# Soft-MoE over a windowed average: first output batch in half sets, later row softmaxes one batch later

## The chip, the cores and the metric

The kernel runs on one core of a Trainium2 chip. The metric is the device time of one execution in microseconds (us), lower is better. The core's engines work side by side and wait for each other through semaphores: TensorE (PE, its weight loads PEld), VectorE (DVE), ScalarE (ACT), GpSimd (POOL) and SyncE (SP), which here issues all loads of the inputs x, w1, w2 and all stores of the output. Sixteen DMA engines move the data. DVE and ACT copy results out of PSUM, the memory that TensorE writes.

## The reference

```
# x: 8 x 3584 x 192, weight: 8 x 7, phi: 192 x 32, w1: 8 x 192 x 1024, w2: 8 x 1024 x 192
w = softmax(weight, axis=-1)                        # one 7-tap filter for each of 8 heads of 24 channels
x = causal_window_sum(w, x).reshape(28672, 192)     # 28672 tokens
logits = x @ phi                                    # 28672 x 32
d = softmax(logits, axis=0)                         # over all tokens
slot_input = (d.T @ x).reshape(8, 4, 192)           # 8 experts, 4 slots each
for e in range(8):
    slot_out[e] = relu(slot_input[e] @ w1[e]) @ w2[e]
c = softmax(logits, axis=1)                         # over the 32 slots of a token
out = c @ slot_out                                  # 28672 x 192, float32
```

## The kernel before

The eight batches of 3584 tokens go through three stages. **Stage 1** (to some 126 us) loads x, filters it on TensorE, forms the logits of all batches (tiles `eb[b]`, 128 partitions by 896) and gathers the slot inputs. **Stage 2** (126 to 143 us) runs the experts: two layers on TensorE, whose result lies in PSUM (`op`, 128 by 2 by 192). It is copied to SBUF in two halves `oc[0]` (DVE) and `oc[1]` (ACT), multiplied with a selector (`gather`) and copied by DVE to `so`, the slot outputs. **Stage 3** (from 143 us) is the output. For a batch b, `c @ slot_out` needs `so` and the row softmax of `eb[b]`, which the key `ct{b}` stands for.

`rows(b)` makes that softmax in eight steps in a row: DVE transpose (L615), DVE minimum (L612), POOL subtraction (L605), ACT exponential (L618), DVE sum (L612), two short DVE steps (L608, L609), POOL multiplication (L605), DVE transpose (L622).

The output of a batch is 4 groups c of 128 rows by 7 tokens q by 192 values. A **set** of the loop at the end of the kernel takes two tokens k, k+1 of all four groups (the fourth set one token): 8 products (16 PE instructions in the profile; 56 for a batch) into two PSUM tiles, c = 0, 1 in the first and c = 2, 3 in the second. Two pairs of PSUM tiles take turns. Each PSUM tile is copied to the output buffer `ob` by ACT or DVE, 768 values wide (L197 for ACT, L201 for DVE). The buffers `ob` of batches 0 to 3 are the former x tiles `rb[1]` to `rb[4]`, used again by batches 4 to 7. After the last set of a batch, SP issues four stores, one for each c, of 7 tokens (672 KB). Batch 0 is cut finer: its first set is copied in four pieces 384 wide and stored at once (four stores of 2 tokens, 192 KB), and the other five tokens follow after the last set (four stores of 480 KB).

The order of the work on each engine is fixed before the run. Every step is given to `Plan.add` with a modelled cost for each engine that could do it, what it reads and writes, and a priority. Steps below priority 1000 are placed first; the rest (the row softmaxes and the output) fill the gaps in the order of their priority, the smaller first. The row softmaxes of batches 0 to 2 have priorities 1100 to 1120, and those of later batches

```python
pr = 1100 + 10 * b if b < 3 else 2000 + 20 * (b - 2) - 1
```

where the output of batch b has 2000 + 20 b + k. So the softmax of batch 3 stands just ahead of the output of batch 1. Waits are put in by the framework, which keeps two engines from working on the same PSUM tile at once.

Of the kernel before, what the change touches and what calls it, by code (L numbers as in the profile page):

```python
# [15 lines left out]
class Plan:  # L16
# [15 lines left out]
    def add(self, fn, cost, reads=(), writes=(), prio=0.0, after=(), chain=False):  # L32

        i = len(self.steps)
        deps = {self.writer[r] for r in reads if r in self.writer}
        if chain:
            if self.last is not None:
                deps.add(self.last)
            self.last = i
        for w in tuple(writes) + tuple(after):  # L40
            if w in self.writer:
                deps.add(self.writer[w])
            deps.update(self.readers.get(w, ()))
        for r in reads:
            self.readers.setdefault(r, []).append(i)
        for w in writes:
            self.writer[w] = i
            self.readers[w] = []
        deps.discard(i)
        self.steps.append((fn, cost, deps, prio))  # L50
# [101 lines left out]
def tile_conv_softmoe(ctx: ExitStack, tc: tile.TileContext, x, weight, phi, w1, w2, out):  # L152
    nc = tc.nc
    P = 128
    B, S, D = x.shape
# [8 lines left out]
    NU = S // T // 2  # L164
# [5 lines left out]
    TQ = NC // P  # L170
# [10 lines left out]
    add = plan.add  # L181

    def act(n):
        return 0.2 + n / 1250

    def dve(n):
        return 0.13 + n / 960

    def pool(n):
        return 0.12 + n * 0.00217  # L190

    def dma(nbytes):
        return {"DMA": nbytes / 320e3}

    def copy(e, dst, src):
        if e == "ACT":
            nc.scalar.copy(dst, src)  # L197
        elif e == "POOL":
            nc.gpsimd.tensor_copy(dst, src)  # L199
        else:  # L200
            nc.vector.tensor_copy(dst, src)  # L201

    def veng(e):
        return nc.gpsimd if e == "POOL" else nc.vector
# [4 lines left out]
    def sb(name, *shape):  # L209
        return cp.tile(list(shape), F32, tag=name, name=name)  # L210

    prs = [pp.tile([P, 2, 512], F32, tag=f"ps{i}", name=f"ps{i}") for i in range(4)]
# [25 lines left out]
    so = sb("so", P, D)  # L238
# [64 lines left out]
    for i in range(5):  # L303
        if i == 1:
# [7 lines left out]
                start=True, stop=True,  # L312
# [32 lines left out]
    for h in range(H):  # L345
# [7 lines left out]
        def bsum(e, prod=prod, h=h):  # L353
# [7 lines left out]
            writes=[f"prod{h}"], prio=-40 + h,  # L361
# [19 lines left out]
    def take():  # L381
        p = state["pair"]
        while p in state["held"]:
            p = (p + 1) % 4
        state["pair"] = (p + 1) % 4
        return p
# [207 lines left out]
            load_x(b + NR)  # L594

    def rows(b):
        pr = 1100 + 10 * b if b < 3 else 2000 + 20 * (b - 2) - 1
        fl = eb[b]
        ev = fl.rearrange("p (q n) -> p q n", n=NS)
        rm = rms[:, b % 2]  # L600
        rb_ = rm.unsqueeze(2).broadcast_to((P, 28, NS))
        ks = [f"e{b}.0", f"e{b}.1"]

        def apply_rows(op):
            return lambda e: veng(e).tensor_tensor(out=ev, in0=ev, in1=rb_, op=op)  # L605

        def recip(e):
            nc.vector.tensor_scalar(out=rm, in0=rm, scalar1=1e-9, scalar2=None, op0=ALU.add)  # L608
            nc.vector.reciprocal(rm, rm)  # L609

        def red(op):
            return lambda e: nc.vector.tensor_reduce(out=rm, in_=ev, axis=AX.X, op=op)  # L612

        rk = f"rm{b % 2}"
        add(lambda e: nc.vector.transpose(fl, fl), {"DVE": dve(NC)}, writes=ks, prio=pr)  # L615
        add(red(ALU.min), {"DVE": dve(NC)}, reads=ks, writes=[rk], prio=pr)
        add(apply_rows(ALU.subtract), {"POOL": pool(NC)}, reads=[rk], writes=ks, prio=pr)
        add(lambda e: nc.scalar.activation(fl, fl, AF.Exp, scale=-1.0), {"ACT": act(NC)}, writes=ks, prio=pr)  # L618
        add(red(ALU.add), {"DVE": dve(NC)}, reads=ks, writes=[rk], prio=pr)
        add(recip, {"DVE": 0.25}, writes=[rk], prio=pr)  # L620
        add(apply_rows(ALU.mult), {"POOL": pool(NC)}, reads=[rk], writes=ks, prio=pr)
        add(lambda e: nc.vector.transpose(fl, fl), {"DVE": dve(NC)}, reads=ks, writes=[f"ct{b}"], prio=pr)  # L622
# [4 lines left out]
    for j, unit in enumerate(units):  # L627
        prev = units[j - 1] if j else []
        for s, b in enumerate(unit):
            between = {}  # L630
            if s == 0 and prev:
                step, done = logits(prev)
                if True:
                    k = 0
# [84 lines left out]
    xh = [xt[:, z].rearrange("p a b c -> p (a b c)") for z in range(2)]  # L719
# [15 lines left out]
    for q in range(4):  # L735
        for z in range(2):
            home, kk = (xh[0], xk0) if z == 0 else (flat(rb[0]), allk(0))
# [6 lines left out]
    for b in range(B):  # L744
        rows(b)

    pr = 300
    pa, pb, pc, pd = (take() for _ in range(4))
    hT = xh[1][:, 2 * NU * 32 : 3 * NU * 32].rearrange("p (q j n) -> p q j n", q=4, n=P)
    hs = xh[1][:, 3 * NU * 32 : 4 * NU * 32].rearrange("p (q f) -> p q f", f=FQ)  # L750
    oc = [xh[1][:, 4 * NU * 32 + a * D : 4 * NU * 32 + (a + 1) * D] for a in range(2)]
# [37 lines left out]
    op = prs[pc][:, 1, 0 : 2 * D].rearrange("p (a d) -> p a d", d=D)  # L789
# [47 lines left out]
    def l2(q):  # L837
        def fn(e):
            for j in range(2):
                for g in range(G):  # L840
                    nc.tensor.matmul(
                        op[g * NS : (g + 1) * NS], hT[:, q, j, g * NS : (g + 1) * NS],
                        w2v[g // 2][:, 2 * (g % 2) : 2 * (g % 2) + 2, q, j, :],
                        start=(q == 0 and j == 0), stop=(q == 3 and j == 1),
                    )

        add(
            fn, {"PE": 1.33}, reads=[f"hT{q}"] + [f"w2.{q}.{z}" for z in range(2)],
            writes=["op"], after=[f"p{pc}"] if q == 0 else [], prio=pr + 1, chain=True,
        )  # L850
# [11 lines left out]
    turn_h(3)  # L862
    for q in range(1, 4):
        l2(q)
    for a in range(2):
        add(
            lambda e, a=a: copy(e, oc[a], op[:, a]), {"ACT": 0.36} if a else {"DVE": 0.33},
            reads=["op"], writes=[f"oc{a}"], after=["dn0.0", "dn0.1"], prio=pr + 4,
        )

    def gather(e):
        for a in range(2):
# [6 lines left out]
    obk = {0: allk(1), 1: allk(2), 2: allk(3) + w1k[0], 3: allk(4) + w1k[1]}  # L879
    obv = [t[:, 0 : 4 * TQ * D].rearrange("p (c q d) -> p c q d", c=4, d=D) for t in sv]  # L880
    nset = 0
    for b in range(B):
        pr = 2000 + 20 * b
        ob = obv[b % 4]
        for k in range(0, TQ, 2):
            qs = range(k, min(k + 2, TQ))
            nq = len(qs)
            v = nset % 2
            q4 = prs[2 * v : 2 * v + 2]
            pk = [f"p{2 * v}", f"p{2 * v + 1}"]  # L890
            nset += 1

            def mm(e, qs=qs, q4=q4, b=b, k=k):
                for q in qs:
                    for c in range(4):
                        sl = slice(32 * c, 32 * c + 32)
                        cb = eb[b][sl].rearrange("p (m q) -> p m q", q=TQ)
                        nc.tensor.matmul(  # L898
                            q4[c // 2][:, c % 2, (q - k) * D : (q - k + 1) * D], cb[:, :, q], so[sl, :],
                            start=True, stop=True, tile_position=(32 * c, 0),  # L900
                        )

            add(
                mm, {"PE": 0.4 * nq}, reads=["so", f"ct{b}"],
                writes=pk + (["op", "ht0", "ht1", "mtb"] if b == 0 else []), prio=pr + k,
            )
            w = 1 if b == k == 0 else 2
            for j in range(4 // w):

                def oev(e, j=j, q4=q4, nq=nq, k=k, ob=ob, w=w):  # L910
                    c0 = j * w
                    copy(
                        e, ob[:, c0 : c0 + w, k : k + nq, :].rearrange("p c q d -> p c (q d)"),
                        q4[c0 // 2][:, c0 % 2 : c0 % 2 + w, 0 : nq * D],
                    )

                add(
                    oev, {"ACT": act(w * nq * D), "DVE": dve(w * nq * D)}, reads=[pk[j * w // 2]],
                    writes=[f"ob{b % 4}.{c}.{k}" for c in range(j * w, j * w + w)],
                    after=obk[b] if b < 4 else [], prio=pr + k,  # L920
                )
            if (b == 0 and k == 0) or k == 6:
                k0 = 2 if b == 0 and k == 6 else 0
                for c in range(4):

                    def st(e, c=c, b=b, ob=ob, k0=k0, k1=k + nq):
                        ih, f = (c // 2, c % 2) if b < NHB else (c % 2, c // 2)
                        base = (b * S + (S // 2) * ih + T * f + k0) * D
                        dst = bass.AP(out.tensor, base, ap=[[2 * T * D, 16], [TQ * D, T // TQ], [1, (k1 - k0) * D]])
                        nc.sync.dma_start(dst, ob[:, c, k0:k1].rearrange("p q d -> p (q d)"))  # L930

                    add(
                        st, dma(P * (k + nq - k0) * D * 4),
                        reads=[f"ob{b % 4}.{c}.{z}" for z in range(k0, k + nq, 2)], prio=pr + k + 4,
                    )

    plan.emit()
# [28 lines left out]
```

## Time and profile before

| what | us |
|---|---|
| median of 3 runs (204.8, 206.45, 208.21) | 206.45 |
| the profiled execution | 207.46 |
| its span from the first to the last instruction | 205.7 |
| TensorE busy in the span | 172.8 |
| VectorE busy | 151.9 |
| ScalarE busy | 100.4 |
| GpSimd busy | 78.2 |

The profiled execution took 1.76 us more than its span. Its PE row counts pipelined matmuls, so a busy PE isn't a PE at its peak. Of 60.08 MB moved, 22.02 MB are the output.

### The profile page before, as it was taken

The numbers are of one execution on the slowest core, as the hardware profiler recorded it, in microseconds if no ns is written. First come the engines' busy times: TensorE is split into PE (matmuls) and PEld (weight loads), VectorE is DVE, ScalarE is ACT, GpSimd is POOL, SyncE is SP. The second block draws the span as 40 slices with busy tenths as digits, with TensorE's granted clock in tenths as the row PEclk, the third lists the DMA queues.
The fourth block names the chain that finished last, engine by engine and source line by source line (L and its number), as shares of the span: only waits on it lengthen the run. The fifth ranks groups of instructions, "written<-read, shape, count | busy, mean of one in ns | idle before, by whom it ended". The sixth has DMA issues, their size and how long they took to land.

```text
span 205.7 us, 6098 instructions
## 1 busy us (share of the span) xinstructions
PE 172.8 (84%) x2610; PEld 104.0 (51%) x2610; DVE 151.9 (74%) x232; ACT 100.4 (49%) x156; POOL 78.2 (38%) x69
## 2 busy tenths in 40 slices
PE   7899899799999899989999999998999989970000
PEld 3367564147433385323632577344889968870000
DVE  5999971399997799959889567869799999760000
ACT  3547750391653845637873080132598878650000
POOL 7555555566665532383000303306336345300000
PEclk9999999999999999999999999999999985695555
DMA  5999999999999819998069799900599999999995
GB/s 163 323 322 330 320 330 321 330 319 316 327 323 323 252 25 291 335 379 185 20 219 317 180 384 376 358 21 0 153 304 331 407 413 412 401 413 417 414 417 211
DMA packets 46124, 60.08 MB, mean 292 GB/s; under 512 B 1682, under 2 KB 38930, under 8 KB 46098
## 3 DMA queue, kind: packets, MB, share of 16 engines
q1 hardware_dynamic: 45888, 59.68, 87.8%
q8 instruction: 20, 0.33, 0.7%
q10 hardware_dynamic: 210, 0.02, 0.1%
q14 instruction: 6, 0.05, 0.1%
HBM read 37.68 MB, written 22.02 MB: 290 GB/s over the span
## 4 chain that ended last, share of the span: by engine, by line
PE 58%; SPq 11%; DMA 8%; DVE 6%; ACT 3%; issue 2%; POOL 1%; DVEq 0%; ACTq 0%
PE ps L403 14%; PE ps L898 14%; PE ps L487 11%; PE ps L578 10%; SPq L271 9%; DMA rb<-in_x_dram 5%; PE ps L553 4%; DMA out_dram<-rb 3%; SPq L267 2%; DVE eb L511 2%; PE ps L795 2%; ACT rb L197 2%; ACT xt L526 2%; DVE rb L201 1%; DVE eb L615 1%
## 5 line engine op out<-in xcount | busy, mean ns | idle before, releaser
L197 ACT COPY rb<-ps 128x768 f32<-128x768 f32 (+1 forms) x98 | 70.1, 778 | 52.5 <-PE ps L403 27.1
L447 DVE STREAM_TRANSPOSE xt<-rb 128x1024 f32<-128x1024 f32 (+1 forms) x60 | 56.9, 1002 | 6.1 <-ACT rb L197 3.9
L199 POOL COPY rb<-rb 8x1536 f32<-8x1536 f32 x30 | 43.7, 1458 | 37.6 <-DMA rb<-in_x_dram 35.1
L403 PE MATMUL ps<-rb,toep 64*64 64x384 f32 (+1 forms) x640 | 48.4, 428 | 2.8 <-issue 1.1
L605 POOL TENSOR_TENSOR eb<-eb,rms 128x896 f32<-128x896 f32 x16 | 27.0, 1696 | 41.5 <-DVE rms L609 37.1
L898 PE MATMUL ps<-so,eb 32*128 32x192 f32 x448 | 39.2, 450 | 2.3 <-ACT rb L197 0.8
L898 PEld LDWEIGHTS ps<-so,eb 32*128 32x128 f32 x448 | 35.6, 317 | 5.9 <-issue 2.2
L403 PEld LDWEIGHTS ps<-rb,toep 64*64 64x64 f32 x640 | 21.9, 132 | 27.4 <-issue 14.8
L487 PE MATMUL ps<-xt,phi 32*32 32x448 f32 x768 | 28.7, 545 | 2.6 <-issue 2.5
L201 DVE COPY rb<-ps 128x768 f32<-128x768 f32 (+1 forms) x32 | 25.1, 816 | 4.2 <-PE ps L898 2.2
L487 PEld LDWEIGHTS ps<-xt,phi 32*32 32x32 f32 x768 | 10.1, 103 | 18.2 <-issue 12.5
L578 PE MATMUL ps<-rb,xt 128*32 128x192 f32 x448 | 19.0, 327 | 0.0
L612 DVE TENSOR_REDUCE rms<-eb 128x28 f32<-128x896 f32 x16 | 17.0, 1065 | 0.0
L578 PEld LDWEIGHTS ps<-rb,xt 128*32 128x32 f32 x448 | 14.1, 110 | 4.0 <-ACT rb L197 0.3
L526 ACT ACTIVATE xt<-eb,nmr 128x896 f32<-128x896 f32 x8 | 8.3, 1044 | 6.5 <-DVE eb L511 6.3
L197 ACT COPY xt<-ps 128x512 f32<-128x512 f32 (+2 forms) x12 | 6.1, 528 | 8.2 <-DVE xt L201 6.8
L553 PE MATMUL ps<-ident,xt 128*128 128x128 f32 x64 | 8.7, 280 | 1.3 <-ACT xt L526 1.2
L553 PEld LDWEIGHTS ps<-ident,xt 128*128 128x128 f32 x64 | 6.9, 141 | 5.6 <-ACT xt L526 3.8
L622 DVE STREAM_TRANSPOSE eb<-eb 128x896 f32<-128x896 f32 x8 | 8.9, 1107 | 0.5 <-POOL eb L605 0.5
L618 ACT ACTIVATE eb<-eb 128x896 f32<-128x896 f32 x8 | 7.6, 955 | 1.9 <-POOL eb L605 1.9
L310 PE MATMUL ps<-ident 128*128 128x512 f32 x10 | 7.4, 888 | 1.4 <-POOL ident masks.py:199 1.4
L615 DVE STREAM_TRANSPOSE eb<-eb 128x896 f32<-128x896 f32 x8 | 8.5, 1081 | 0.0
(90 smaller groups left out, 111.7 us busy)
## 6 DMA issues: line engine op xcount, KB each, us to landing
out_dram<-rb SPq DMA_DIRECT2D x28, 672.0 KB, 9.0
rb<-in_x_dram SPq DMA_DIRECT2D x24, 768.0 KB, 9.5
rb<-in_x_dram SPq DMA_DIRECT2D x8, 672.0 KB, 7.3
rb<-in_moe_w_dram SPq DMA_DIRECT2D x4, 1024.0 KB, 9.2
xt<-in_moe_w_dram SPq DMA_DIRECT2D x4, 768.0 KB, 6.0
rb<-in_moe_w_dram SPq DMA_DIRECT2D x4, 768.0 KB, 10.7
rb<-in_moe_w_dram SPq DMA_DIRECT2D x4, 512.0 KB, 13.2
out_dram<-rb SPq DMA_DIRECT2D x4, 480.0 KB, 6.2
```

The costliest lines, as they stand in the source:

```text
L197: nc.scalar.copy(dst, src)
L199: nc.gpsimd.tensor_copy(dst, src)
L201: nc.vector.tensor_copy(dst, src)
L271: nc.sync.dma_start(rb[i][:, u0 : u0 + k, :], src)
L403: nc.tensor.matmul(dst[:, :, h * CG : (h + 1) * CG], toep[r, h0 + h, :], rb[i][r, lo + g : lo + n : 2, ch], start=True, stop=True,)
L447: nc.vector.transpose(xt[:, s, k, lo : lo + n], rb[i][:, lo : lo + n, 32 * k : 32 * k + 32])
L487: nc.tensor.matmul(q[a % 2][32 * c : 32 * c + 32, a // 2, 0 : m * U * TH].rearrange("p (s u j) -> p s u j", s=m, j=TH), phi4[sl, k, :], xt ...
L553: nc.tensor.transpose(q[:, u // 4, (u % 4) * P : (u % 4 + 1) * P], t[:, u].rearrange("p g t -> p (g t)"), ident)
L578: nc.tensor.matmul(q[32 * c : 32 * c + 32, 0, 0:D], d[:, u, 32 * c : 32 * c + 32], rb[i][:, U * c + u, :], start=(u == 0), stop=(u == U - 1),)
L605: return lambda e: veng(e).tensor_tensor(out=ev, in0=ev, in1=rb_, op=op)
L612: return lambda e: nc.vector.tensor_reduce(out=rm, in_=ev, axis=AX.X, op=op)
L898: nc.tensor.matmul(q4[c // 2][:, c % 2, (q - k) * D : (q - k + 1) * D], cb[:, :, q], so[sl, :], start=True, stop=True, tile_position=(32 * ...
```

## The change

There are three edits. The output of batch 0 is made in four half sets: c = 0, 1 with tokens 0 to 3, c = 2, 3 with tokens 0 to 3, then the same with tokens 4 to 6. In a half set the first PSUM tile holds the first two tokens and is copied by ACT, the second holds the rest and is copied by DVE, one copy for each c. Each c is stored as soon as its tokens of the half set are copied: four stores of 4 tokens (384 KB) and four of 3 tokens (288 KB), in place of four of 2 and four of 5. Secondly, the row softmax of a batch b from 3 on gets the priority just ahead of batch b-1 instead of b-2. Thirdly, the expert result is copied out of PSUM by one DVE copy of 384 values in place of a DVE and an ACT copy of 192.

```diff
     def rows(b):
-        pr = 1100 + 10 * b if b < 3 else 2000 + 20 * (b - 2) - 1
+        pr = 1100 + 10 * b if b < 3 else 2000 + 20 * (b - 1) - 1
...
-    for a in range(2):
-        add(
-            lambda e, a=a: copy(e, oc[a], op[:, a]), {"ACT": 0.36} if a else {"DVE": 0.33},
-            reads=["op"], writes=[f"oc{a}"], after=["dn0.0", "dn0.1"], prio=pr + 4,
-        )
+    add(
+        lambda e: nc.vector.tensor_copy(xh[1][:, 4 * NU * 32 : 4 * NU * 32 + 2 * D], prs[pc][:, 1, 0 : 2 * D]),
+        {"DVE": 0.53}, reads=["op"], writes=["oc0", "oc1"], after=["dn0.0", "dn0.1"], prio=pr + 4,
+    )
...
-        for k in range(0, TQ, 2):
-            qs = range(k, min(k + 2, TQ))
-            nq = len(qs)
+        if b:
+            sets = [(range(4), k, min(k + 2, TQ)) for k in range(0, TQ, 2)]
+        else:
+            sets = [((c, c + 1), k, min(k + 4, TQ)) for k in (0, 4) for c in (0, 2)]
+        for cs, k, k1 in sets:
...
+            def home(c, q, q4=q4, b=b, k=k):
+                t, j = (c // 2, c % 2) if b else ((q - k) // 2, c % 2)
+                return q4[t][:, j, (q - k) % 2 * D : ((q - k) % 2 + 1) * D]
...
+                parts = [
+                    (ob[:, c, z : min(z + 2, k1), :].rearrange("p q d -> p (q d)"), q4[(z - k) // 2][:, c % 2, 0 : (min(z + 2, k1) - z) * D],
+                     (min(z + 2, k1) - z) * D, (z - k) // 2, (c,), z, ("ACT", "DVE")[(z - k) // 2])
+                    for c in cs for z in range(k, k1, 2)
+                ]
...
-            if (b == 0 and k == 0) or k == 6:
-                k0 = 2 if b == 0 and k == 6 else 0
-                for c in range(4):
+            if b == 0 or k1 == TQ:
+                for c in cs:
```

How this moves instructions is shown at three places. In the rows below, eb_73 to eb_80 are the logits of batches 0 to 7, rb_68 to rb_71 the four output buffers, ps_63 to ps_66 the four PSUM tiles. The first place is VectorE at the end of stage 2, the difference of the two orders.

```order
 L615 STREAM_TRANSPOSE eb_78<-eb_78 128x896
-L201 COPY xt<-ps_66 128x192
+L866 COPY xt<-ps_66 128x384
 L622 STREAM_TRANSPOSE eb_75<-eb_75 128x896
-L876 COPY so<-ps_65 128x192
+L875 COPY so<-ps_65 128x192
 L612 TENSOR_REDUCE rms<-eb_77 128x28
```

The copy of the expert result is twice as wide there; between it and the copy to `so` stands, as before, the last softmax step of batch 2. The second place is VectorE in the output of batches 0 and 1, before:

```order
L201 COPY rb_68<-ps_63 128x384
L201 COPY rb_68<-ps_64 128x384
L201 COPY rb_68<-ps_66 128x2x384
L201 COPY rb_68<-ps_64 128x2x384
L201 COPY rb_68<-ps_66 128x2x192
L612 TENSOR_REDUCE rms<-eb_76 128x28
L608 TENSOR_SCALAR rms<-rms 128x28
L609 RECIPROCAL rms<-rms 128x28
L201 COPY rb_69<-ps_65 128x2x384
L615 STREAM_TRANSPOSE eb_79<-eb_79 128x896
L622 STREAM_TRANSPOSE eb_76<-eb_76 128x896
L201 COPY rb_69<-ps_65 128x2x192
```

and with the change:

```order
L201 COPY rb_68<-ps_64 128x384 x2
L201 COPY rb_68<-ps_66 128x384 x2
L201 COPY rb_68<-ps_64 128x192 x2
L201 COPY rb_68<-ps_66 128x192 x2
L201 COPY rb_69<-ps_64 128x2x384
L201 COPY rb_69<-ps_66 128x2x384
L201 COPY rb_69<-ps_64 128x2x384
L201 COPY rb_69<-ps_66 128x2x192
L612 TENSOR_REDUCE rms<-eb_76 128x28
L608 TENSOR_SCALAR rms<-rms 128x28
L609 RECIPROCAL rms<-rms 128x28
L201 COPY rb_70<-ps_65 128x2x384
```

The sum of batch 3 (eb_76) and what follows it now stand behind the copies of batch 1 (rb_69) and among those of batch 2 (rb_70). The third place is SP's stores of the first batches, before:

```order
L280 DMA rb_67<-in_moe_w_dram 128x4x384
L930 DMA out_dram<-rb_68 16x8x384 x4
L930 DMA out_dram<-rb_68 16x8x960 x4
L930 DMA out_dram<-rb_69 16x8x1344 x4
L930 DMA out_dram<-rb_70 16x8x1344 x4
```

and with the change:

```order
L280 DMA rb_67<-in_moe_w_dram 128x4x384
L936 DMA out_dram<-rb_68 16x8x768 x4
L936 DMA out_dram<-rb_68 16x8x576 x4
L936 DMA out_dram<-rb_69 16x8x1344 x4
L936 DMA out_dram<-rb_70 16x8x1344 x4
```

Batch 0 has eight stores in both; the last number is the values of one row, 768 for 4 tokens and 576 for 3.

## Rows read from the trace of the kernel before

**Rows 1.** Page, part 2: GB/s moved in 40 slices of 5.14 us.

```profile
GB/s 163 323 322 330 320 330 321 330 319 316 327 323 323 252 25 291 335 379 185 20 219 317 180 384 376 358 21 0 153 304 331 407 413 412 401 413 417 414 417 211
```

**Rows 2.** Windows of stage 3: busy us of each engine, clock, DMA share, GB/s.

```profile
144.80:149.10 4.30, 3.92 (x52) 3.46 (x50) 3.81 (x6) 2.33 (x4) 0.78 (x1) 1.00 0.61 183
149.10:153.70 4.60, 4.51 (x59) 4.06 (x56) 4.50 (x8) 4.39 (x7) 1.70 (x1) 1.00 0.98 317
153.70:157.50 3.80, 3.80 (x50) 3.55 (x46) 3.65 (x6) 3.59 (x6) 1.20 (x1) 1.00 0.91 278
157.50:202.00 44.50, 25.11 (x284) 22.68 (x282) 24.05 (x33) 19.90 (x29) 10.58 (x7) 0.69 1.02 411
```

**Rows 3.** Windows of one microsecond each, with the same columns.

```profile
145.00:146.00 1.00, 0.71 (x10) 0.58 (x8) 1.00 (x3) 0.95 (x2) 0.58 (x1) 1.00 0.00 0
146.00:147.00 1.00, 1.00 (x20) 1.00 (x18) 0.69 (x1) 0.26 (x1) 0.00 (x0) 1.00 0.81 218
148.00:149.00 1.00, 1.00 (x16) 1.00 (x18) 1.00 (x3) 0.00 (x0) 0.00 (x0) 1.00 0.91 300
152.00:153.00 1.00, 0.91 (x8) 0.69 (x6) 0.97 (x2) 1.00 (x3) 0.01 (x1) 1.00 0.98 376
```

**Rows 4.** Timeline, SP's stores: start, us, and at the end how many remain.

```profile
144.83 50.51 SPq L930 DMA_DIRECT2D out_dram<-rb  x36
...
146.87 48.47 SPq L930 DMA_DIRECT2D out_dram<-rb  x33
...
147.95 47.40 SPq L930 DMA_DIRECT2D out_dram<-rb  x32
...
153.74 41.60 SPq L930 DMA_DIRECT2D out_dram<-rb  x28
...
159.00 36.34 SPq L930 DMA_DIRECT2D out_dram<-rb  x24
```

**Rows 5.** Chain that ended last, 141 to 152 us: start, us, what.

```profile
141.06 0.36 DVE xt L201
141.42 1.02 DVE eb L622
...
142.46 0.37 DVE so L876
...
142.96 1.32 PE ps L898 x16
...
144.29 0.49 ACT rb L197
...
144.80 0.57 DVE rb L201
...
147.68 4.68 PE ps L898 x55
```

**Rows 6.** Timeline, DVE in the output of batch 1.

```profile
148.51 1.08 DVE L612 TENSOR_REDUCE rms<-eb 128x28 f32<-128x896 f32 x1
149.62 0.18 DVE L608 TENSOR_SCALAR rms<-rms 128x28 f32<-128x28 f32 x1
149.84 0.33 DVE L609 RECIPROCAL rms<-rms 128x28 f32<-128x28 f32 x1
...
150.91 1.10 DVE L615 STREAM_TRANSPOSE eb<-eb 128x896 f32<-128x896 f32 x1
152.04 1.11 DVE L622 STREAM_TRANSPOSE eb<-eb 128x896 f32<-128x896 f32 x1
153.07 0.52 DVE L201 COPY rb<-ps 128x384 f32<-128x384 f32 x1
```

**Rows 7.** Groups by form from 142.9 us: count, busy us, mean ns, idle before.

```profile
L605 POOL TENSOR_TENSOR eb<-eb,rms 128x896 f32<-128x896 f32 x9 | 15.2, 1695 | 19.5 <-DVE rms L609 18.1 <-DVE rms L612 1.3
L201 DVE COPY rb<-ps 128x768 f32<-128x768 f32 x15 | 13.9, 942 | 3.2 <-PE ps L898 2.2 <-issue 0.8
...
L201 DVE COPY rb<-ps 128x384 f32<-128x384 f32 x10 | 5.1, 532 | 1.0 <-ACT rb L197 1.0
```

More of the change, by code (lines that the diff above doesn't have):

```diff
@@ L891, in tile_conv_softmoe, with mm @@
             nset += 1
-            def mm(e, qs=qs, q4=q4, b=b, k=k):
-                for q in qs:
-                    for c in range(4):
+            def home(c, q, q4=q4, b=b, k=k):
+                t, j = (c // 2, c % 2) if b else ((q - k) // 2, c % 2)
+                return q4[t][:, j, (q - k) % 2 * D : ((q - k) % 2 + 1) * D]
+            def mm(e, cs=cs, b=b, k=k, k1=k1, home=home):
+                for q in range(k, k1):
+                    for c in cs:
                         sl = slice(32 * c, 32 * c + 32)
@@ L898, in mm @@
                         nc.tensor.matmul(
-                            q4[c // 2][:, c % 2, (q - k) * D : (q - k + 1) * D], cb[:, :, q], so[sl, :],
-                            start=True, stop=True, tile_position=(32 * c, 0),
+                            home(c, q), cb[:, :, q], so[sl, :], start=True, stop=True, tile_position=(32 * c, 0),
                         )
             add(
-                mm, {"PE": 0.4 * nq}, reads=["so", f"ct{b}"],
+                mm, {"PE": 0.8}, reads=["so", f"ct{b}"],
@@ L905, in tile_conv_softmoe @@
                 writes=pk + (["op", "ht0", "ht1", "mtb"] if b == 0 else []), prio=pr + k,
             )
[L907 to L915, printed above, removed]
-                add(
-                    oev, {"ACT": act(w * nq * D), "DVE": dve(w * nq * D)}, reads=[pk[j * w // 2]],
-                    writes=[f"ob{b % 4}.{c}.{k}" for c in range(j * w, j * w + w)],
-                    after=obk[b] if b < 4 else [], prio=pr + k,
-                )
@@ L922, in tile_conv_softmoe @@
-            if (b == 0 and k == 0) or k == 6:
-                k0 = 2 if b == 0 and k == 6 else 0
-                for c in range(4):
-                    def st(e, c=c, b=b, ob=ob, k0=k0, k1=k + nq):
+            if b:
+                n = (k1 - k) * D
+                parts = [
+                    (ob[:, 2 * j : 2 * j + 2, k:k1, :].rearrange("p c q d -> p c (q d)"), q4[j][:, :, 0:n], 2 * n, j, (2 * j, 2 * j + 1), k, None)
+                    for j in range(2)
+                ]
+            else:
+                parts = [
+                    (ob[:, c, z : min(z + 2, k1), :].rearrange("p q d -> p (q d)"), q4[(z - k) // 2][:, c % 2, 0 : (min(z + 2, k1) - z) * D],
+                     (min(z + 2, k1) - z) * D, (z - k) // 2, (c,), z, ("ACT", "DVE")[(z - k) // 2])
+                    for c in cs for z in range(k, k1, 2)
+                ]
@@ new lines, in tile_conv_softmoe, with st @@
+            for dst, src, m, t, pcs, z, eng in parts:
+                cost = {"ACT": act(m), "DVE": dve(m)}
+                add(
+                    lambda e, dst=dst, src=src: copy(e, dst, src), {eng: cost[eng]} if eng else cost, reads=[pk[t]],
+                    writes=[f"ob{b % 4}.{c}.{z}" for c in pcs], after=obk[b] if b < 4 else [], prio=pr + k,
+                )
+            if b == 0 or k1 == TQ:
+                for c in cs:
+                    def st(e, c=c, b=b, ob=ob, k0=0 if b else k, k1=k1):
@@ L930, in st @@
                         nc.sync.dma_start(dst, ob[:, c, k0:k1].rearrange("p q d -> p (q d)"))
+                    k0 = 0 if b else k
                     add(
-                        st, dma(P * (k + nq - k0) * D * 4),
-                        reads=[f"ob{b % 4}.{c}.{z}" for z in range(k0, k + nq, 2)], prio=pr + k + 4,
+                        st, dma(P * (k1 - k0) * D * 4),
+                        reads=[f"ob{b % 4}.{c}.{z}" for z in range(k0, k1, 2)], prio=pr + k + 4,
                     )
```

## The prediction, made before the change was run

> **What bounds the kernel now.** I read the page by slices first. From 160 us to the end the core moves 401 to 417 GB/s slice after slice, and nothing else is left but the output; in the four slices from 144 us it is 153, 304, 331 and 407 [rows 1]. So stage 3 is bound by the stores once they run full, and its loss lies at its head. The windows give the size of it: 183, 317 and 278 GB/s in three stretches from 144.8 to 157.5 us, then 411 for 44.5 us, while the DMA engines are at 1.02 of their time [rows 2]. Computation isn't the bound later: from 157.5 on PE, DVE and ACT are busy 25.1, 24.1 and 19.9 of 44.5 us [rows 2].
>
> Next I read the issues of the stores. The first leaves at 144.83 us, the fifth (5 tokens) at 147.95, the ninth (batch 1) at 153.74, the thirteenth (batch 2) at 159.00 [rows 4]. Nothing moves before 146 us [rows 3], so some 1.3 us lie between an issue and its data. Batch 0 is 22.02/8 = 2.752 MB, and at 411 GB/s that is 6.70 us; from 146.1 it could be gone by 152.8, but its bytes come late (0.79 MB in the first four stores) and batch 1's data start only at 153.74 + 1.3 = 155.0. Up to 157.5 us the kernel has moved 4.3 x 183 + 4.6 x 317 + 3.8 x 278 = 3301 KB [rows 2].
>
> The chain before it shows what sets the first store: DVE's copy of the expert result (0.36), the last softmax step of batch 2 (1.02), `so` (0.37), 16 PE instructions (1.32), one ACT copy (0.49) [rows 5]. DVE's own first copy starts only when ACT's has ended, 144.80 against 144.29 + 0.49 [rows 5].
>
> **The change, part by part.** *One copy of the expert result.* The DVE copy is 384 wide, 0.53 us by the group of that width [rows 7] in place of 0.36. The ACT copy goes, but `gather` doesn't set the time: behind the DVE copy stands the transpose of batch 2 and behind that `so`, all on DVE without a gap [rows 5]. So `so` comes 0.17 us later, not sooner, and PE's first output product starts at 142.96 + 0.2 = 143.15. Bounds: 0 if the transpose had been waiting for something else, 0.21 with the 0.57 of the chain's DVE copy [rows 5]. I take 0.2.
>
> *Half sets.* Batch 0 keeps its 56 PE instructions, 1.32/16 = 82 ns each [rows 5]: half sets of 16, 16, 12 and 12 end at 144.5, 145.8, 146.8 and 147.8. A store needs an ACT and a DVE copy, now out of different PSUM tiles, so neither waits for the other. The DVE copy is the later one, for its tile is filled last: 144.5 + 0.55 gives the first store at 145.1, 0.25 later than before but with 384 KB in place of 192. The copies rise from 10 to 16 in batch 0, which costs 2 x 532 - 942 = 122 ns for a pair on DVE [rows 7]; they lie beside PE, which needs 1.0 to 1.3 us for a half set against two copies of 0.53 us on DVE and two of like length on ACT (0.49 for one [rows 5]). SP sends the first four in (146.87 - 144.83)/3 = 0.68 us each [rows 4], so the eight leave between 145.1 and 149.9; before, the four heavier ones left only from 147.95 on [rows 4].
>
> How fast do they move? Rows of 2 tokens move 300 GB/s at a share of 0.91, rows of 5 tokens 376 at 0.98 [rows 3], which is 330 and 384 GB/s at full share. Rows of 4 and 3 tokens lie between: 2.752 MB take 7.2 to 8.3 us from 145.1 + 1.3 = 146.4, and batch 0 is gone between 153.6 and 154.7.
>
> Here a rule speaks against any gain. The Trainium skill, "DMA: Bandwidth & Descriptors", section "Anatomy of one DMA", fits a DMA as a fixed 2.0 us plus its bytes at 436 GB/s (there for GpSimd's path), and "Rules for kernel authors" asks for 1 MiB or more in each. By that fit batch 0's eight stores cost an estimated 22.3 us before and after alike, since count and bytes stay, and nothing would be won. The trace speaks against a serial fixed cost: 218 to 300 GB/s went by while four stores of 192 KB followed each other 0.68 us apart [rows 3, 4].
>
> *Row softmaxes one batch later.* Before, DVE does steps of batches 3 and 4 around its first copy of batch 1, from the sum at 148.51 to the transpose that starts at 152.04 and takes 1.11 us, and batch 1's last copy starts only then, at 153.07 [rows 6]; its store leaves at 153.74. Now batch 1's copies are alone. But PE sets them nearly as late: 56 instructions at 4.68/55 = 85 ns [rows 5] are 4.8 us, from 147.8 to 152.5. The last copy (0.53) follows, and the ninth store leaves at 153.1, 0.65 us sooner; its data start at 154.4. So most of the DVE time that is freed is not on the path: PE is next, at 0.65 us. The steps aren't saved, only moved behind it: sum, two short steps, transpose (1.11) [rows 6] and POOL's product (1.70) [rows 7] are now due before batch 3, and the last copy of batch 2 stands behind that transpose.
>
> **The sum.** By 157.5 us the changed kernel has moved batch 0's 2752 KB, and from 154.4 on 3.1 us of batch 1. If that runs as slowly as the restart did before, at 278 GB/s, it is 862 KB; if at 411, 1274 KB [rows 2]. That makes 3614 to 4026 KB against 3301, so 313 to 725 KB less are left, and at 411 GB/s that is 0.76 to 1.76 us. I take the middle, 1.26 us, as batch 0's data end within 0.8 us of batch 1's start on either side. After that both kernels run full. The profiled execution took 207.46 us, 1.76 more than its span of 205.7, and nothing of the change touches that: 206.2. It lies 1.0 above the median of 206.45, so against the median I forecast 206.45 - 1.26 = 205.2 us.
>
> **The rivals.** *No gain (206.1).* Batch 1's stores are due where they were, because PE or the last copies hold them: then its data start at 155.0, and by 157.5 there are 2752 + 2.5 x 278 = 3447 KB, 146 more, or 0.36 us. For it: PE ends batch 1 at 152.4 before (147.68 + 4.68) and 152.5 after, and the first copy is later. Against: the row of the last copy, which stood idle for DVE's transpose [rows 6]. The page's fit above would land here too.
>
> *Full from the start (203.4).* Batch 0 runs at 411 GB/s from 146.4 and batch 1 joins without a seam: 11.1 x 411 = 4562 KB by 157.5, 1261 more, 3.07 us. For it: the issue pace of 384 KB in 0.68 us is 578 GB/s, more than the engines take. Against: rows 3, where shorter rows move less at the same share, and the first stretch, which never ran full.
>
> *Slower (207.7).* The softmax of batch 3 arrives late and starves the queue. The last DVE copy of batch 2, which two of its stores wait for, comes behind a sum (1.08), two short steps (0.51), a transpose of batch 4 (1.10) and batch 3's own (1.11), which waits for POOL's 1.70 [rows 6, 7], and a copy (0.94). From 153.05 that is 157.8 and the copy ends at 158.3. The queue has batch 1 until 154.4 + 6.7 = 161.1, so these stores must leave by 159.8: a margin of 1.5 us. A slip of 1.5 + 1.26 = 2.8 us eats the gain; with 4 us it is 206.45 + 1.2. For it: GpSimd's and ACT's steps in that chain wait for DVE, and DVE is at 0.98 of its time in the second stretch [rows 2]. Against: before, the same chain stood in front of batch 1 and the queue was empty then; now it has a full batch more. Later there is room: after 157.5 us DVE and ACT are busy for little more than half of the time [rows 2], so a chain that begins one batch's 4.8 us of PE later need not bind.
>
> **How the numbers follow.** The forecast has a chance of 0.58, no gain 0.22, full 0.12, slower 0.08. The likeliest is 205.2. The three runs of before lie 1.7 us to either side of their median, more than the bounds of the sum; with the rivals' ends the range is 203.1 to 207.0, which leaves out the slower case and the far ends of noise. A measurement of this kernel tells about 2% (4.1 us) from no change. The whole loss at the head is 12.7 x 411 - 3301 = 1919 KB, 4.7 us, and 1.3 us of it pass before the first data, so faster by over 2% needs more than there is to win: 0.03. Slower by 2% needs the starving of the third rival three times over: 0.03. Within 2%: 0.94.
>
> **What would show it.** Right: the first store at 145.1, the ninth near 153.1, the thirteenth before 159.8; above 1.2 MB by 149.1 and some 3.8 MB by 157.5 us; 411 GB/s from there on; PE's first output product 0.2 us later. DVE's copies of batch 0 no longer wait for ACT's. Wrong in the first step: the ninth store at 153.7 or later, with PE waiting for PSUM. Wrong in the second: the four-token stores move under 300 GB/s, or the rate falls again at batch 1 as it did at 153.7. Wrong in the last: a dip of GB/s after 161 us with SP waiting for a DVE copy behind L622.

## The result, and the profile after

The changed kernel takes 207.99 us against 206.79 for the kernel before, medians of 20 runs each: a ratio of 1.006 (95% interval 1.0035 to 1.0084). It is slower by 0.6%, where 0.6% faster was forecast, and 207.99 lies outside the range of 203.1 to 207.0. The profiled execution took 208.68 us, its span is 206.9. The ratios compare runs within 1.5% of each kernel's fastest one; since single runs scatter by as much, the table of the experiments has the medians of all runs beside them, and a difference that only one of the two says is called open.

The page of the changed kernel, part 2, the rows of the clock and of GB/s:

```profile
PEclk9999999999999999999999999999799975587555
...
GB/s 162 324 320 329 321 329 321 329 320 321 324 321 328 226 35 316 341 352 166 19 276 288 207 378 373 313 9 0 124 333 304 417 408 415 413 402 415 414 414 211
```

From the slice at 160 us on the rate is what it was [rows 1]: the tail still runs full. The loss lies in the slices from 144 us (124, 333, 304 against 153, 304, 331), and PEclk, the granted clock of TensorE in tenths, has a 7 there. The windows of stage 3, with the bounds of [rows 2]:

```profile
144.80:149.10 4.30, 4.22 (x54) 3.98 (x52) 2.57 (x6) 3.10 (x8) 0.95 (x1) 0.67 0.31 76
149.10:153.70 4.60, 4.55 (x62) 4.34 (x64) 3.83 (x6) 2.81 (x5) 0.00 (x0) 1.00 1.01 343
153.70:157.50 3.80, 3.80 (x53) 3.44 (x52) 3.68 (x7) 3.00 (x5) 1.70 (x1) 1.00 0.96 293
157.50:202.00 44.50, 25.46 (x282) 22.36 (x280) 25.61 (x34) 22.87 (x35) 11.84 (x7) 0.70 1.01 406
```

By 157.5 us it has moved 4.3 x 76 + 4.6 x 343 + 3.8 x 293 = 3018 KB, against 3301 before and 3614 to 4026 forecast. The start of the last window is slow as well. The changed kernel, and below it the kernel before:

```profile
157.50:160.50 3.00, 2.01 (x34) 1.96 (x32) 3.00 (x4) 2.62 (x5) 0.00 (x0) 1.00 0.98 330
160.50:202.00 41.50, 23.45 (x252) 20.41 (x248) 22.61 (x31) 20.25 (x31) 11.84 (x7) 0.67 1.02 412
```

```profile
157.50:160.50 3.00, 3.00 (x44) 2.92 (x42) 2.77 (x4) 2.28 (x4) 2.15 (x2) 1.00 1.01 403
160.50:202.00 41.50, 22.11 (x246) 19.75 (x244) 21.28 (x30) 17.62 (x26) 8.43 (x5) 0.67 1.02 412
```

That is (403 - 330) x 3.0 = 219 KB behind 157.5 us, on top of the 3301 - 3018 = 283 KB before it. Together 502 KB are 1.22 us at 411 GB/s, as much as lies between the two profiled executions (208.68 - 207.46), and about the 1.20 between the medians. Single microseconds of the changed kernel:

```profile
147.00:148.00 1.00, 1.00 (x18) 0.97 (x12) 0.79 (x2) 0.60 (x2) 0.00 (x0) 0.68 0.34 80
148.00:149.00 1.00, 0.92 (x13) 0.71 (x12) 0.76 (x3) 0.99 (x3) 0.00 (x0) 1.00 0.87 203
...
157.00:158.00 1.00, 0.55 (x8) 0.31 (x4) 0.95 (x2) 1.00 (x2) 0.25 (x1) 1.00 1.03 221
160.00:161.00 1.00, 1.00 (x17) 0.80 (x13) 0.96 (x2) 1.00 (x2) 0.00 (x0) 1.00 1.01 414
```

A share of 0.34 in the first of these says that data starts at about 147.66 us. The microsecond at 157 stands where batch 1's 7-token rows, whose first store left at 154.96 us (below), take over from batch 0's 3-token rows: the DMA engines are busy throughout (1.03), and move 221 GB/s. At 160 us the rate is full.

SP's stores, in the columns of [rows 4], are the first, fourth, fifth, eighth, ninth and thirteenth:

```profile
146.46 49.01 SPq L936 DMA_DIRECT2D out_dram<-rb  x36
...
148.76 46.71 SPq L936 DMA_DIRECT2D out_dram<-rb  x33
...
149.88 45.59 SPq L936 DMA_DIRECT2D out_dram<-rb  x32
...
153.20 42.27 SPq L936 DMA_DIRECT2D out_dram<-rb  x29
...
154.96 40.51 SPq L936 DMA_DIRECT2D out_dram<-rb  x28
...
159.78 35.69 SPq L936 DMA_DIRECT2D out_dram<-rb  x24
```

The first leaves 1.4 us later than forecast (145.1) and 1.6 later than before. The chain that ended last (start, us, what) says why:

```profile
140.99 0.56 DVE xt L866
141.54 1.02 DVE eb L622
...
142.62 0.37 DVE so L875
...
143.13 4.06 PE ps L903 x38
...
147.21 1.03 DVE rb L201 x2
...
148.29 4.10 PE ps L903 x54
...
152.41 1.42 DVE rb L201 x2
```

Between `so` and the next copy it has only PE. VectorE's timeline of the same stretch, with its idle time and who ended it in brackets:

```profile
145.75 1.02 DVE L201 COPY rb<-ps 128x384 f32<-128x384 f32 x2 [1.78 <-PE ps L903]
147.21 1.55 DVE L201 COPY rb<-ps 128x384 f32<-128x384 f32 x4 [0.44 <-PE ps L903]
```

VectorE stands idle for 1.78 us, and what ends that is PE: the first half set's 16 instructions took from 143.13 to 145.75, 2.62 us, where the 16 of the first set took 1.32 before [rows 5].

### The profile page after: what moved, and what is told of

It reads as the page before. It is cut to its first block, busy times and chain, and to the rows that moved or that the text cites. A ratio compares the mean times of both kernels' runs of the same rounds, so it can differ in the third digit from the quotient of the medians.

```text
span 206.9 us, 6095 instructions
## 1 busy us (share of the span) xinstructions
PE 173.9 (84%) x2610; PEld 104.4 (50%) x2610; DVE 151.7 (73%) x233; ACT 101.6 (49%) x160; POOL 78.4 (38%) x69
## 4 chain that ended last, share of the span: by engine, by line
PE 53%; DVE 12%; SPq 11%; DMA 5%; POOL 4%; ACT 4%; issue 3%; DVEq 0%; ACTq 0%; POOLq 0%
PE ps L403 14%; PE ps L487 11%; PE ps L903 10%; PE ps L578 9%; SPq L271 9%; DMA rb<-in_x_dram 5%; PE ps L553 4%; POOL eb L605 3%; DVE rb L201 3%; DVE rms L612 2%; SPq L267 2%; DVE eb L622 2%; DVE eb L511 2%; ACT rb L197 2%; PE ps L795 2%
## 5 line engine op out<-in xcount | busy, mean ns | idle before, releaser
L197 ACT COPY rb<-ps 128x768 f32<-128x768 f32 (+1 forms) x103 | 71.2, 757 | 56.7 <-PE ps L403 32.7
L903 PE MATMUL ps<-so,eb 32*128 32x192 f32 x448 | 39.7, 476 | 7.8 <-DVE eb L622 6.5
L201 DVE COPY rb<-ps 128x768 f32<-128x768 f32 (+2 forms) x33 | 24.8, 776 | 9.3 <-PE ps L903 8.2
L622 DVE STREAM_TRANSPOSE eb<-eb 128x896 f32<-128x896 f32 x8 | 8.8, 1106 | 0.1
L197 ACT COPY xt<-ps 128x512 f32<-128x512 f32 (+1 forms) x11 | 5.8, 548 | 4.7 <-DVE xt L201 3.3
```

The source lines that it names most:

```text
L903: nc.tensor.matmul(home(c, q), cb[:, :, q], so[sl, :], start=True, stop=True, tile_position=(32 * c, 0),)
```

## The experiments

In the table, the times of the first and the ninth store are counted from PE's first output product, and so is the mean rate over 25 us from there on (windows of each trace); the medians are those of all runs of the kernel and of the kernel before, taken side by side on one chip for each experiment. In e6, which has four stores fewer, the ninth store is batch 2's first; batch 1's first is the fifth, at +10.53.

| kernel | ratio (95% interval) | medians, this and before | first store | ninth | GB/s |
|---|---|---|---|---|---|
| before | 1 | | +1.87 | +10.78 | 302 |
| changed | 1.006 (1.0035 to 1.0084) | 207.99, 206.79 | +3.33 | +11.83 | 286 |
| e1, rows later | 0.9957 (0.9901 to 1.0014) | 207.66, 207.47 | +1.87 | +9.63 | 307 |
| e2, half sets | 1.0072 (1.0028 to 1.0117) | 207.84, 207.47 | +3.15 | +11.67 | 291 |
| e9, one copy | 1.002 (0.9979 to 1.0062) | 207.80, 207.16 | +1.88 | +11.16 | 298 |
| e3, four groups | 0.9981 (0.994 to 1.0021) | 206.70, 207.47 | +2.91 | +10.81 | 296 |
| e7, token order | 1.0035 (0.9999 to 1.0071) | 207.67, 207.35 | +2.91 | +11.37 | 295 |
| e5, order in a set | 1.0012 (0.997 to 1.0053) | 207.56, 207.23 | +1.88 | +10.81 | 307 |
| e4, batch 1 as 4 + 3 | 1.0117 (1.0061 to 1.0174) | 209.14, 207.47 | +1.87 | +9.15 | 274 |
| e6, only 7 tokens | 1.0073 (1.0034 to 1.0112) | 208.38, 207.23 | +5.03 | +16.50 | 285 |
| e8, own tiles | 0.996 (0.9919 to 1.0002) | 206.93, 207.16 | +1.87 | +9.20 | 310 |

**The change taken apart: e1, e2 and e9.** Each is the kernel before with one of the three edits: e1 has the new priority of the row softmaxes, e2 the half sets with their copies and stores (the part of the diff from `sets` on), e9 the one copy of the expert result.

```diff
-        pr = 1100 + 10 * b if b < 3 else 2000 + 20 * (b - 2) - 1
+        pr = 1100 + 10 * b if b < 3 else 2000 + 20 * (b - 1) - 1
```

> The kernel before with the later row softmaxes alone. Theory: the half sets of batch 0 cost the time, since TensorE runs two of four row groups there; the later softmaxes are a small gain. Then the ninth store leaves at 153.0 to 153.4 us and the time is 0.5 to 1.3 us under the kernel before (ratio 0.994 to 0.998). Rival: the later softmaxes starve a later batch; then the ratio is about 1.006, with a dip of GB/s after 161 us.

> The kernel before with the half sets of batch 0 and their stores alone; softmaxes and expert copies as before. Theory: the first half set takes 2.6 us on TensorE as in the changed kernel, the first store leaves at 146.2 to 146.4 us and the ninth at 155 or later, 207.8 to 209 us (ratio 1.005 to 1.011). Rival (late softmaxes at fault): ratio 1.000 or under.

> The kernel before with one copy of the expert result alone. Every theory: the copy to so and TensorE's first output product come some 0.2 us later after the copy's start (2.1 in place of 1.9 us), ratio 1.000 to 1.002. A ratio of 1.004 or over would put part of the loss here.

The loss goes with the half sets, as far as it can be told from the noise: e2's first store comes 1.28 us later than before, and over the 25 us its rate is 11 GB/s lower, 275 KB or 0.67 us at 411. Its ratio is above 1 with its interval, though its median is only 0.37 us higher; the ratios of e1 and e9 aren't told from 1. Later softmaxes bring the ninth store 1.15 us forward, but no gain that stands out (e1's ratio and its medians differ in sign). One copy moves PE's first product: from the copy's start to that product are 144.00 - 141.86 = 2.14 us in e9, as in the changed kernel (143.13 - 140.99), and 142.96 - 141.06 = 1.90 before [rows 5]; in the time of the kernel that is lost in the noise. VectorE in e9:

```profile
141.86 0.56 DVE L866 COPY xt<-ps 128x384 f32<-128x384 f32 x1
142.34 1.10 DVE L622 STREAM_TRANSPOSE eb<-eb 128x896 f32<-128x896 f32 x1
143.50 0.36 DVE L875 COPY so<-ps 128x192 f32<-128x192 f32 x1
```

**Is it that only two row groups work? e3 and e7.** A half set has two of the four values of c, so its instructions use two of the four groups of 32 rows of PE. e3 is the changed kernel, but two half sets are computed together, four values of c in turn; tiles, copies and stores stay (the planner's cost of the step is 0.65). e7 keeps the half sets and only goes through their tokens as 0, 2, 1, 3, so that four PSUM banks are written in turn.

```diff
+            if not b and cs[0] == 0:
+                def mm4(e, k=k, k1=k1):
+                    for q in range(k, k1):
+                        for c in range(4):
...
+                            t = 2 * (c // 2) + (q - k) // 2
...
-                for q in range(k, k1):
+                for q in range(k, k1) if b else sorted(range(k, k1), key=lambda q: ((q - k) % 2, q)):
```

> The changed kernel with the products of two half sets of batch 0 run together, the four groups c in turn for each token; tiles, copies and the stores of 4 and 3 tokens stay. Theory: TensorE is back at 82 ns an instruction. The first store is as late as in the changed kernel (146.3 us), since 32 instructions stand before it, but batch 0's last product ends about 0.6 to 1.3 us sooner, the ninth store leaves by 154.2 and the time is 0.7 to 1.4 us under the changed kernel, 206.6 to 207.3. Rival (stores of 4 and 3 tokens move slowly whatever TensorE does): 208.0, as the changed kernel.

> The changed kernel with the tokens of a half set in the order 0, 2, 1, 3, so that its products go to four PSUM banks in turn (two in each of its two tiles) in place of two; the two row groups, the copies and the stores stay. Theory A: a row group works its instructions off one by one, some 0.23 us each, and a half set keeps only two of four busy; then nothing changes, the DVE's first output copy starts about 2.6 us after TensorE's first output product, and the time is that of the changed kernel (ratio to the kernel before 1.003 to 1.009). Theory B: it is the PSUM bank that takes one product at a time; then that copy starts about 1.4 to 1.7 us after, the first store leaves 1 us sooner, and the ratio is 0.996 to 1.002.

Windows of 1.1 us from the first product, PE's instructions of the output line alone (PE, PEld, clock, share, GB/s). The changed kernel:

```profile
143.10:144.20 1.10, 1.07 (x9) 1.10 (x10) 1.00 0.00 0
144.20:145.30 1.10, 1.10 (x16) 1.10 (x16) 0.51 0.00 0
```

The kernel before:

```profile
142.90:144.00 1.10, 1.04 (x16) 1.07 (x20) 1.00 0.00 0
```

e3, four groups in turn:

```profile
143.30:144.40 1.10, 1.10 (x20) 1.10 (x21) 1.00 0.00 0
```

e7, other tokens and banks, two groups:

```profile
141.70:142.80 1.10, 1.07 (x9) 1.10 (x10) 1.00 0.00 0
```

VectorE's first copies in e7, whose first product is at 141.73 us:

```profile
143.93 1.02 DVE L201 COPY rb<-ps 128x384 f32<-128x384 f32 x2 [1.36 <-PE ps L903]
```

That is 2.20 us after the first product, sooner than theory A had it (2.6) and later than theory B (1.4 to 1.7). The granted clock falls later in e7 than in the changed kernel, which the account of the prediction comes back to.

At a granted clock of 1.00 PE starts 9 instructions with two groups and 16 to 20 with four. The banks are no reason: with four of them e7 still starts 9. The Trainium skill, "TensorEngine Tiling (Array Packing)", sections "Overview" and "Tiling Modes", has tiles work independently and in parallel, with up to 4x for four of them; by that, two in flight give half the pace, and the trace agrees (9 against 16 to 20). The slow pace doesn't last, though. The changed kernel's second window has 16 at half the clock, and e7, whose clock is still at 1.00 there, has 19 in its own:

```profile
142.80:143.90 1.10, 1.10 (x19) 1.10 (x18) 1.00 0.00 0
```

That is the pace of four groups again, while e7's first half set isn't done before 143.9 us (VectorE's first copy above). So the second half set, on the other two groups, runs beside the rest of the first: the half sets delay the first finished piece, more than they slow PE as a whole.

The ratios of the changed kernel and of e3 are 0.8% apart (1.006 / 0.9981, by medians 1.0058 / 0.9963), about 1.6 us, and their intervals don't meet. In the profiles 250 KB of that are seen by 25 us (296 against 286 GB/s), 0.6 us; e3's own profiled execution took 208.49 us, 1.8 above its median, so no spans are compared. But e7, with two groups, moves 295 GB/s in these 25 us, as much as e3, its ratio of 1.0035 lies between, and its interval meets both. And e3 brings back not only the groups: its clock stays at 1.00 where that of the changed kernel falls to 0.51. So the groups are shown to set the pace of the first half set; how much of the 0.6% is theirs is not shown.

Yet e3's first store leaves as late as e7's, at +2.91: with four groups at full pace, 32 instructions must end before the first 4-token store can leave; with two at half pace, 16. Its first store is 1.04 us later than that of before, and still it isn't slower than the kernel before; so a late first store is not by itself the loss. What e3 gains on the changed kernel comes behind that: the ninth store leaves at +10.81, not +11.83.

**Does the order within a set count? e5.** The kernel before, with both tokens of a c behind each other, so that each pair of products (four PE instructions) has the same row group.

```diff
-                for q in qs:
-                    for c in range(4):
+                for c in range(4):
+                    for q in qs:
```

> The kernel before with the products of every set in another order: all tokens of group c = 0, then of 1, 2, 3, in place of the four groups in turn for each token; nothing else changes. Theory: products of different row groups run side by side on TensorE and those of one group one after the other, so the first set of 16 instructions goes from 1.3 to about 3 us, a batch from 4.6 to 9 to 12 us, TensorE becomes the bound of the output and the time rises to 225 to 245 us. Rival (the order of the groups is of no matter to TensorE, the half set was slow through its PSUM tiles): 206 to 208 us.

That expectation fell: 1.0012, and 18 instructions in the first 1.1 us:

```profile
143.60:144.70 1.10, 1.09 (x18) 1.10 (x19) 1.00 0.00 0
```

So a short run on one group costs nothing, while all four come within eight products. PE runs ahead into the other groups: the first four instructions of the program are of one group there, yet four start in the first 0.06 us of the trace, as in the kernel before, and two in the changed kernel and in e7, whose half sets have two groups. The trace doesn't name the group of an instruction, so this is read from the number that start together.

**What is an earlier byte worth? e6 and e4.** e6 is e1 with only 7-token stores: the orders of the computing engines are those of e1, and batch 0 is stored after its last set. e4 is e1 with batch 1, whose stores meet a queue that already runs, stored in 4 and 3 tokens.

```diff
-            if (b == 0 and k == 0) or k == 6:
-                k0 = 2 if b == 0 and k == 6 else 0
+            if (b == 0 and k == 0) or (b == 1 and k == 2) or k == 6:
+                k0 = (2, 4)[b] if b < 2 and k == 6 else 0
```

> The later row softmaxes alone, with batch 0 stored like the others, four stores of 7 tokens after its last set; the order on DVE, ACT and PE is the same as in that kernel. Data start about 3.7 us later. Theory A: rows shorter than 7 tokens, and the change from one row length to another, are what slows the head; then it runs at about 411 GB/s soon after its first data, has 5.2 MB or more moved 20 us after TensorE's first output product, and the time is within 0.5 us of the later softmaxes alone (ratio to the kernel before 0.993 to 0.999). Theory B: the head is slow after any start, and early bytes are worth their time; then 1.5 to 3.7 us slower (ratio 1.003 to 1.014).

> The later softmaxes alone, and batch 1 stored in 4 tokens after its second set and 3 after its last; batch 0 as before. Theory: batch 1's first bytes leave at about 151.5 us, before batch 0's have gone, so that the queue never runs dry: 204.5 to 205.8 us (ratio 0.989 to 0.996). Rival (rows of 4 and 3 tokens are what costs): no better than the later softmaxes alone, or 0.5 us slower than those.

In e6 the first store leaves 3.16 us later than in e1. At 411 GB/s that would be 1.3 MB; the windows of 25 us differ by 22 GB/s, 550 KB or 1.3 us. Against the kernel before, whose first store leaves as early as e1's, the ratio says 1.5 us, the medians 1.2. So of each microsecond some half or less was paid for, as theory B of the expectation had it. The Trainium skill's page "DMA: Bandwidth & Descriptors", section "Anatomy of one DMA", has a fixed 2.0 us in each DMA (there for GpSimd's path); if SP's stores paid as much, one after the other, an estimated 8 us would be saved with the four stores fewer. The run doesn't agree: it is slower. e6 in windows, from the last microsecond without data on:

```profile
146.00:147.00 1.00, 1.00 (x20) 1.00 (x22) 0.46 (x1) 0.03 (x1) 0.00 (x0) 1.00 0.00 0
147.00:148.00 1.00, 1.00 (x22) 1.00 (x18) 0.66 (x1) 0.94 (x2) 0.00 (x0) 1.00 1.03 226
148.00:149.00 1.00, 1.00 (x18) 1.00 (x16) 1.00 (x2) 0.63 (x1) 0.00 (x0) 1.00 0.87 188
149.00:150.00 1.00, 1.00 (x16) 0.82 (x12) 0.57 (x2) 0.78 (x2) 0.00 (x0) 1.00 1.06 323
150.00:151.00 1.00, 0.90 (x10) 0.87 (x12) 1.00 (x3) 0.40 (x2) 0.00 (x0) 1.00 0.91 355
151.00:155.00 4.00, 3.79 (x52) 3.38 (x48) 3.89 (x7) 3.27 (x5) 1.70 (x1) 1.00 1.01 407
```

Even 7-token rows, at a share of 0.87 to 1.06, start with 226 and 188 GB/s and are full only in the fifth microsecond. Still they are the fastest of all once they run: over 9.84 us from the first data e6 moves 358 GB/s, e1 291. And e4 shows what a change of the row's length does in the middle of a running queue:

```profile
155.00:157.00 2.00, 1.01 (x15) 0.79 (x12) 1.95 (x4) 2.00 (x4) 0.31 (x1) 1.00 0.91 341
157.00:159.00 2.00, 2.00 (x34) 1.80 (x32) 1.97 (x3) 1.61 (x3) 0.00 (x0) 1.00 0.96 363
159.00:161.00 2.00, 2.00 (x24) 1.73 (x24) 1.44 (x4) 1.79 (x4) 1.41 (x1) 1.00 0.96 308
161.00:163.00 2.00, 0.23 (x6) 0.12 (x4) 2.00 (x3) 0.88 (x4) 1.94 (x2) 0.78 0.96 313
163.00:165.00 2.00, 2.00 (x25) 2.00 (x29) 1.06 (x2) 1.25 (x2) 1.18 (x1) 0.50 1.00 298
165.00:167.00 2.00, 2.00 (x28) 1.68 (x25) 1.93 (x4) 1.53 (x3) 0.52 (x1) 0.50 1.00 366
167.00:169.00 2.00, 1.52 (x16) 1.02 (x8) 1.53 (x3) 1.98 (x4) 1.66 (x1) 0.50 1.02 382
169.00:171.00 2.00, 0.75 (x8) 0.75 (x12) 2.00 (x3) 0.49 (x1) 0.04 (x1) 0.50 1.00 409
```

The 4- and 3-token rows run at 341, 363 and 308, and for some 8 us more the rate stays under 409, with the engines busy. Over the 25 us e4 moves 33 GB/s less than e1, 825 KB or 2.0 us, and its ratio to the kernel before says 1.2%, 2.4 us (1.7 by the medians, of 6 runs). My own expectation of e4 missed. The rival had the direction, and its 0.5 us over e1 became 1.5 by the medians. So the first short rows paid for themselves in e1 against e6, and the further ones of e4 did not.

**First copies from tiles of their own: e8.** e1, and in the first set ACT copies both pieces of one PSUM tile and VectorE both of the other.

```diff
-                    oev, {"ACT": act(w * nq * D), "DVE": dve(w * nq * D)}, reads=[pk[j * w // 2]],
+                    oev, {("ACT", "DVE")[j // 2]: act(nq * D)} if w == 1 else {"ACT": act(w * nq * D), "DVE": dve(w * nq * D)},
+                    reads=[pk[j * w // 2]],
```

> The later row softmaxes, batch 0 stored in 2 and 5 tokens as before, and the first set copied with one engine to each PSUM tile (ACT c = 0, 1, DVE c = 2, 3), so that DVE's first copy no longer waits for ACT's. Theory: TensorE keeps its four row groups, the first store still leaves 1.9 us after the first output product, DVE's copies start 0.5 us sooner, and the later softmaxes' small gain shows: 0.994 to 0.999 of the kernel before. Rival: the later softmaxes gain nothing, 1.000 and over.

VectorE's wait for ACT's copy [rows 5] is gone, and its first copy starts 0.5 us sooner after PE's first product (+1.34, not +1.84). The ninth store comes earlier than in e1, at +9.20, but the time is 0.996 of before, no better than e1's, and 1 is within the interval. The experiments thus point to no version that is clearly faster than the kernel before.

## Why the prediction was wrong

**One copy** was right: 0.2 us forecast; 2.14 against 1.90 us is 0.24.

**Half sets: the step that failed first** is "Batch 0 keeps its 56 PE instructions, 1.32/16 = 82 ns each". The 82 ns hold for instructions that go round all four row groups. A half set has two, and its first 16 instructions take 2.62 us: 1.3 us on the first store, which the other seven and the data inherit (147.66, not 146.4). e7 excludes the banks. e3, which brings back the four groups, and with them the clock, is no slower than the kernel before; what each of the two is worth in the 0.6% stays open, as said above. The row that I took it from [rows 5] is a run with all four. In these 2.62 us the fall of the granted clock to half, 1.2 of 2.4 GHz, takes part: it came 1.10 us after the first product. In e7 it came 2.8 us after it, behind the first half set, and VectorE's first copy at 143.93 - 141.73 = 2.20. So by this pair, an estimate, some 0.4 of the 1.3 us are the clock's, and the rest the groups'.

**Rate of the head: the second step.** 4- and 3-token rows should move 330 to 384 GB/s. From 147.66 to 157.5 us it was 3018 KB in 9.84 us, 307 GB/s, and part of that was batch 1's. The bounds came from single microseconds in the midst of batch 0, scaled to a full share; they left out that the first ones move less at a full share (203 GB/s at 0.87, then 353 at 1.02 by 150 us), and that the change to the next length of row costs again (221 at 1.03 at 157). e6 and e4 show both apart from the half sets. This also takes the point out of the edit itself. Over 9.84 us from the first data the changed kernel moves 308 GB/s at a share of 0.98, the kernel before 289 at 0.92:

```profile
147.70:157.54 9.84, 9.71 (x124) 8.86 (x118) 8.61 (x16) 7.25 (x13) 1.70 (x1) 1.00 0.98 308
```

```profile
146.10:155.94 9.84, 9.66 (x118) 8.83 (x120) 9.19 (x14) 7.81 (x12) 1.70 (x1) 1.00 0.92 289
```

At a full share both are 314: rows of 4 and 3 tokens are not faster than rows of 2 and 5, the queue only has fewer gaps. That is worth 19 x 9.84 = 187 KB, 0.45 us, and the data start 1.6 us later.

**The ninth store** left at 154.96, not 153.1. PE was on time: the chain has it end at 148.29 + 4.10 = 152.39, where 152.5 was forecast. Behind it VectorE had two copies to make, not one, until 152.41 + 1.42 = 153.83. But the ninth left only 1.1 us after those copies: SP's record of the eighth store runs from 153.20 for 1.66 us, to 154.86. So the copies were not what held it; the stores ahead of it were behind, by the two steps above. The term that I had from the row softmaxes was there: 1.15 us in e1, more than the 0.65 forecast. What it is worth in time is not told from the noise (e1's ratio 0.9957, by the medians 1.0009).

**The sum.** In place of 3820 KB (the middle) 3018 were moved by 157.5, which is 802 KB or 1.95 us. The forecast had 411 GB/s from there on, and until 160.5 it was 330: (411 - 330) x 3.0 = 243 KB, 0.59 us. Together that is 2.5 us, as much as the 1.24 + 1.26 between the measured loss (0.6% of 206.79) and the forecast gain. Another 0.34 us of the distance from 205.2 to 207.99 are the kernel before, 206.79 in 20 runs and 206.45 in the three shown.

**The rivals.** The slower one came near in its time (207.7) by luck, for its mechanism was wrong: no starving. PE's waiting for the transpose L622 stands in the page:

```profile
L903 PE MATMUL ps<-so,eb 32*128 32x192 f32 x448 | 39.7, 476 | 7.8 <-DVE eb L622 6.5
```

These 6.5 us cost no store, as the rate stays above 400 GB/s from 160 us on; the thirteenth store left at 159.78, just inside the margin (159.8), while batch 1 was still under way. No rival spoke of PE's pace; one that asked which row groups the 16 instructions of [rows 5] use would have.

## What to carry to other kernels

Where small matmuls go round row groups, the time of one instruction holds only for that round: a piece of work that is cut by row group gets slower per instruction until the next piece runs beside it, and the first finished piece may come no sooner than with all groups and twice the work (+2.91 for the first store in e7 and in e3). Here the sets cut by what each group streams (tokens) had their first store at +1.87. And before an earlier start of a store queue is given its full rate, read how fast the queue is in its first microseconds: here an earlier microsecond brought less than a half of one.

## What was not expected of the hardware

After the half sets began, the granted clock of TensorE fell to 0.5 (1.2 GHz): in the changed kernel 1.10 us after the first output product, in e2 after 1.5 and in e7 after 2.8. In the kernel before, in e1, e3, e4, e5, e6 and e8 it stayed at 1.00 for at least 15 us from there. But e9, which has no half sets, fell as well, after 5.6 us, so the half sets aren't shown to be its only cause, and no run here settles it. Open too is what makes the rate dip where a queue starts or the length of its rows changes; the runs show the size (188 to 226 GB/s at a share of 0.87 to 1.03), not the reason.
